# Turning x by DMA, starting the first expert units beside expert 0, pacing the weight loads, and loading expert 0's weights in fp32

## The chip, the core and the metric

The kernel runs on one NeuronCore of a Trainium2 chip. The metric is the device time of one execution in microseconds; the time of a version is the median of several runs. The engines named here are TensorE (PE in the profile, with PEld for its weight loads), VectorE (DVE), ScalarE (ACT), GpSimd (POOL) and SyncE (SP), which issues DMAs. POOL and ACT issue DMAs too, and a DMA that converts fp32 to fp16 on its way is issued by POOL in this kernel.

## The reference

Attention with a window of 32 and 32 global tokens, over 8 batches of 8 heads with 512 local tokens; its output, 4352 tokens of 512 numbers, goes through a mixture of eight experts with Sinkhorn routing.

```python
x = attention(q_l, k_l, v_l, q_g, k_g, v_g)      # [4352, 512], tokens b*544 + (32 global, 512 local)
P = np.exp(x @ w_gate)                           # [4352, 8]
for _ in range(8):
    P /= P.sum(1, keepdims=True); P /= P.sum(0, keepdims=True); P *= N / E
for e in range(8):
    out += P[:, e:e+1] * (np.maximum(x @ w1[e], 0) @ w2[e])   # w1: 512x1024, w2: 1024x512
```

Since P is positive, a token's row of x may be scaled by P before expert e's first product.

## The kernel before, in words

**The order of the work** is written by a small planner, not by hand. `op(...)` records an operation with its engine, an assumed duration, what it depends on and a key. `run_schedule` simulates the engines and emits the operation that can start first, the smaller key first among equals. Each engine then runs its instructions in that fixed order, and so does each queue of DMA issues; a late operand holds up everything behind it on the same engine.

**Front: attention.** 32 pairs of heads, four in a batch. For a pair: loads on SP's queue (`load`), casts to fp16 on DVE, eight PE transposes of q and k, evacuations, scores, exponentials on ACT, masks on DVE, `attend` on PE, and `normalise` on DVE (L297), which leaves the pair's output `xn` with tokens on partitions. The later products need x with its 512 features on partitions. So `back` (L329) turns the pair with four PE transposes into PSUM (`gbank`), a copy (L200) brings it to `xT`, one tile that holds x of all tokens, and `flip` (L335) with a copy at L527 does the same for the global tokens. `gate` (L339) multiplies x by w_gate, `exp_gate` writes K_nat.

**Expert 0** is computed densely and unscaled with fp16 weights in `w1_0` and `w2_0`, which two converting DMAs on POOL's queue load (`load_w0`, L540, behind a small POOL copy `tick` that waits for a q load of batch 1). Its units are the filler: `h_unit` (L388) makes one 128-feature slice of h for a group of 512 tokens, `y_unit` (L407) one 128-token slice of y, with keys from 1000, so that PE takes them wherever attention leaves it free. There are 560 such matmuls. y goes to DRAM (`y0d`, L422, on POOL's queue).

**Routing** is a chain of DVE steps with one small PE matmul in each of the eight rounds (L643 to L659, `colsum` L656). It starts when all gates are done and ends in P_nat. P is then turned on PE (L672) and stored to DRAM (`ptd`, L677), and x is stored from `xT` to `xTd` (L610).

**Back: experts 1 to 7.** The tokens are 17 groups of 256. Pass 0 runs experts 1, 2, 3 over all groups, pass 1 experts 4 to 7: 119 units (`work`). A unit is one expert on one group, by a scheme that needs seven block products in place of eight, for each of the two layers: `product1` (P1 to P7 of layer 1, eight matmuls of 128 columns each, L726) and `product2` (L764, four matmuls of 256 columns each). For a unit, `prep` on DVE scales x by P (two operations at L708, from `xg` and `pb`, which `load_group` L690 brings on SP's queue: x of the group, and the P of each expert broadcast to all partitions) and makes the sums `tt` (L97, L100). ACT copies partial sums out of PSUM (`snap`, L737) and does the relus (L740); DVE combines them. In layer 2 the accumulators in PSUM start from the output so far (`load_o` L771, `seed`), and `fin_...` and `store_o` (L936, SP's queue) end a group. `xp`, the scaled x of a unit, has three buffers; P3 is the last product that reads it, in the order written 6.2 + 3.53 us after its unit's P1.

**Weights of experts 1 to 7** come by converting DMAs on POOL's queue, four of 512 KB (written) for an expert: `load_w1` and `load_w2` (L85, L93). Experts 1 and 2 load during attention, 3 when attention's buffers are released, 4 and 5 early in pass 0. Experts 6 and 7 take the buffers of 1 and 2, so their loads wait for the last units of pass 0. `combine_w1` and `combine_w2` make sums of weight blocks on DVE.

The back is scheduled in a second call of `run_schedule`: its first unit is emitted after the last operation of expert 0, and only the `prep` of units 0 and 1 belongs to the first call.

Of the kernel before, what the change touches and what calls it, by code (L numbers as in the profile page):

```python
# [17 lines left out]
def kernel(  # L18
# [51 lines left out]
    identity32 = persist.tile([P, P], FP32)  # L70
    xT = fill.tile([P, DP, NTOK], FP16, bufs=1)
# [6 lines left out]
    xTd = dram.tile([GN, P, DP, 256], FP16)  # L78
    ws = {}

    def load_w1(e, pool, tag=""):
        w1r = pool.tile([P, 4, DK, F // 2], FP16, tag="w1r" + tag, bufs=1, name="w1r")
        src = moe_w1[e].rearrange("(dko dki) f -> dki dko f", dki=P)
        for f in (0, 1):
            nc.gpsimd.dma_start(out=w1r[:, 2 * f : 2 * f + 2].rearrange("p a k x -> p (a k) x"),  # L85
                                in_=src[:, :, F // 2 * f : F // 2 * (f + 1)])
        ws[e] = [w1r, None, None]

    def load_w2(e, pool, tag=""):
        wb = ws[e][1] = pool.tile([P, 7, FK, Dhalf], FP16, tag="wb" + tag, bufs=1, name="wb")  # L90
        src = moe_w2[e].rearrange("(fko fki) d -> fki fko d", fki=P)
        for c in (0, 1):
            nc.gpsimd.dma_start(out=wb[:, 2 * c : 2 * c + 2].rearrange("p a k x -> p (a k) x"),  # L93
                                in_=src[:, :, Dhalf * c : Dhalf * (c + 1)])
# [101 lines left out]
    qkT, ugk, u_, xns, ogs, pts, pss, pgs, pos_, pqs, hTs, phs, pys = ({} for _ in range(13))  # L196
# [100 lines left out]
    def normalise(p):  # L297
# [3 lines left out]
        t = xns[p] = wk.tile([P, NM, 2, Dh], FP16, tag="xn", bufs=3, name="xn")  # L301
# [4 lines left out]
    xo = gbank[:, 0:256].bitcast(FP16)  # L306
    ptg = gbank[:, 384 : 384 + 2 * Sg].rearrange("p (a s) -> p a s", s=Sg)
# [15 lines left out]
    def normalise_g(b, hh):  # L323
        rg = wk.tile([P, 1], FP32, tag="rg", name="rg")
        nc.vector.reciprocal(out=rg, in_=pog[:, Dh:VC])
        t = ogs[b, hh] = wk.tile([P, Dh], FP16, tag="og", name="og")
        nc.vector.tensor_scalar(out=t, in0=pog[:, 0:Dh], scalar1=rg[:, 0:1], scalar2=None, op0=ALU.mult)

    def back(p):  # L329
        for m in range(NM):  # L330
            nc.tensor.transpose(xo[:, P * m : P * (m + 1)], xns[p][:, m, :, :], identity)
# [7 lines left out]
    def gate(t0, t1):  # L339
        for to in range(t0, t1):  # L340
# [610 lines left out]
    for u in range(NW + 2):  # L951
# [10 lines left out]
        if 2 <= u < NW:  # L962
            add_prep(u)
# [31 lines left out]
```

## Time and profile before

| | |
|---|---|
| median of 3 runs | 1023.87 us (1021.98 to 1028.93) |
| the profiled execution: own time, span | 1021.38 us, 1019.7 us |
| mean granted TensorE clock | 0.990 |
| PE busy, PEld busy | 980.2 us (96%), 829.9 us (81%) |
| DVE, ACT, POOL busy | 884.6 us (87%), 671.7 us (66%), 51.8 us (5%) |
| moved by DMA | 119.18 MB, mean 117 GB/s |

The span runs from the first to the last instruction; the 1.7 us between it and the execution's own time lie around it. PE's busy time is modelled, since matmuls overlap in the array: an engine that is busy all the time may still start fewer matmuls than it could. The number of matmuls in a stretch says more.

### The profile page before, as it was taken

The page shows a single profiled execution, that of the slowest core. Times are in us where ns is not written, and L with a number is a line of the kernel's source. Part 1 is how long each engine was busy: PE and PEld are TensorE (multiplying, and loading weights), DVE is VectorE, ACT ScalarE, POOL GpSimd, SP SyncE. Part 2 cuts the span into 40 slices and gives each one's busy share as a digit, 9 for nine tenths or more (in the row PEclk, how much of TensorE's full clock was granted, in tenths as well). Part 3 has the DMA queues.
Part 4 walks back from the last instruction along what each step waited for, and adds up shares of the span by engine and source line. Part 5 has one row for each costly group of instructions (what it writes and reads, how often), then busy time and mean ns, then how long its engine had stood idle before and what let it go on. Part 6 is the DMA issues. An engine that isn't in the chain of part 4 may idle for free. (4 is left out here: it accounts for less than half of the span.)

```text
span 1019.7 us, 30644 instructions
## 1 busy us (share of the span) xinstructions
PE 980.2 (96%) x12921; PEld 829.9 (81%) x12921; DVE 884.6 (87%) x2058; ACT 671.7 (66%) x1306; POOL 51.8 (5%) x89
## 2 busy tenths in 40 slices
PE   5999999889999999999999889999999999999997
PEld 3556555434799999999999878999999999999997
DVE  5577776581599999999999899999999999999996
ACT  4678877434677766676776656666666666666664
POOL 2000130211300000000000100000000000000000
PEclk9799999989999999999999999999999999999999
DMA  9979696732962232232322891222222222222211
GB/s 272 256 219 307 193 215 126 144 103 100 229 140 85 94 94 89 90 94 93 108 73 79 153 195 60 88 73 74 74 74 73 75 74 74 74 75 73 75 43 43
DMA packets 127530, 119.18 MB, mean 117 GB/s; under 512 B 17424, under 2 KB 102944, under 8 KB 127392
## 3 DMA queue, kind: packets, MB, share of 16 engines
q1 hardware_dynamic: 99040, 91.13, 29.3%
q0 software_dynamic: 26768, 25.70, 13.4%
q8 instruction: 101, 1.65, 0.7%
q10 hardware_dynamic: 1584, 0.39, 0.2%
q14 instruction: 37, 0.30, 0.1%
HBM read 102.65 MB, written 31.33 MB: 131 GB/s over the span
## 5 line engine op out<-in xcount | busy, mean ns | idle before, releaser
L740 ACT ACTIVATE h<-h 128x512 f16<-128x512 f16 x357 | 224.2, 630 | 72.0 <-DVE h L100 70.1
L726 PEld LDWEIGHTS <-w1r 128*128 128x128 f16 x3808 | 244.9, 98 | 22.6 <-issue 13.7
L726 PEld LDWEIGHTS <-w1x 128*128 128x128 f16 x2856 | 182.3, 98 | 5.3
L764 PEld LDWEIGHTS <-s 128*128 128x128 f16 x1904 | 172.4, 98 | 15.9 <-DVE s L100 0.6
L708 DVE TENSOR_TENSOR xp<-xg,pb 128x512 f16<-128x512 f16 x238 | 163.0, 686 | 15.2 <-PE Y L726 15.0
L726 PE MATMUL X<-tt,w1r 128*128 128x128 f16 x1904 | 145.1, 219 | 7.4 <-ACT u3s L737 5.8
L764 PE MATMUL acc_4639<-wb,s 128*128 128x256 f16 x952 | 142.5, 273 | 0.3 <-DVE s L100 0.3
L764 PEld LDWEIGHTS <-h 128*128 128x128 f16 x1428 | 130.0, 98 | 12.6 <-issue 1.0
L737 ACT COPY u3s<-X 128x512 f32<-128x512 f32 x119 | 69.4, 583 | 73.7 <-PE X L726 73.4
L100 DVE TENSOR_TENSOR h<-p1s,Z 128x512 f16<-128x512 f32 x119 | 81.0, 681 | 29.5 <-ACT p1s L737 27.9
L737 ACT COPY p1s<-X 128x512 f32<-128x512 f32 x119 | 69.1, 580 | 29.1 <-PE X L726 29.1
L100 DVE TENSOR_TENSOR h<-u3s,Y 128x512 f16<-128x512 f32 x119 | 81.1, 681 | 2.1 <-ACT u3s L737 2.1
L737 ACT COPY u2s<-X 128x512 f32<-128x512 f32 x119 | 68.5, 576 | 21.5 <-PE X L726 21.4
L100 DVE TENSOR_TENSOR h<-u2s,Y 128x512 f16<-128x512 f32 x119 | 81.0, 680 | 1.6 <-PE Y L726 1.6
L740 ACT ACTIVATE h<-X 128x512 f16<-128x512 f32 x119 | 70.1, 589 | 17.0 <-PE X L726 14.0
L396 PE MATMUL ph<-xT,w_0_77 128*128 128x512 f16 (+1 forms) x288 | 74.0, 374 | 1.8 <-ACT ys L200 1.1
L726 PE MATMUL X<-xp,w1r 128*128 128x128 f16 x952 | 72.6, 219 | 1.9 <-DVE xp L708 1.7
L726 PE MATMUL Z<-xp,w1r 128*128 128x128 f16 x952 | 72.6, 219 | 1.1 <-DVE h L100 1.0
L726 PE MATMUL X<-tt,w1x 128*128 128x128 f16 x952 | 72.6, 219 | 0.0
L726 PE MATMUL Y<-tt,w1x 128*128 128x128 f16 x952 | 72.6, 219 | 0.0
L726 PE MATMUL Y<-xp,w1x 128*128 128x128 f16 x952 | 72.6, 219 | 0.0
L764 PE MATMUL acc_4636<-wb,s 128*128 128x256 f16 x476 | 71.4, 273 | 0.1
(985 smaller groups left out, 1651.1 us busy)
## 6 DMA issues: line engine op xcount, KB each, us to landing
pb<-ptd SPq DMA_DIRECT2D x119, 128.0 KB, 4.1
y0d<-ys POOLq DMA_DIRECT2D x34, 256.0 KB, 3.5
xg<-xTd SPq DMA_DIRECT2D x34, 256.0 KB, 3.7
o<-y0d SPq DMA_DIRECT2D x34, 256.0 KB, 2.8
ya<-o SPq DMA_DIRECT2D x34, 256.0 KB, 2.1
o<-ya SPq DMA_DIRECT2D x34, 256.0 KB, 3.0
out_dram<-o SPq DMA_DIRECT2D x34, 256.0 KB, 2.0
qs<-in_q_l_dram SPq DMA_DIRECT2D x7, 1024.0 KB, 6.9
```

Source lines behind the costliest of these rows:

```text
L100: nc.vector.tensor_tensor(out=o, in0=a, in1=b_, op=ALU.add)
L396: nc.tensor.matmul(phs[g, fm][:, 0:TG], w1_0[:, dk, P * fm : P * (fm + 1)], xT[:, dk, P * g0 : P * g0 + TG], start=(dk == 0), stop=(dk == ...
L708: nc.vector.tensor_tensor(out=x[:, ks], in0=xgs[n, g][:, ks], in1=pb.unsqueeze(1).broadcast_to([P, DK, 256]), op=ALU.mult)
L726: nc.tensor.matmul(dst[:, j, :], l[:, d, P * j : P * (j + 1)], r[:, d, :], start=(first and j == 0 and d == 0), stop=(j == FK - 1 and d == ...
L737: nc.scalar.copy(out=d[k], in_=X[k])
L740: nc.scalar.activation(out=hq(k, f, t), in_=hq(k, f, t) if src is None else src, func=AF.Relu)
L764: nc.tensor.matmul(acc(i), l[:, j, :], wb[:, r, j, :], start=(e == es[0] and j == 0 and i in (1, 5)), stop=(e == es[-1] and j == FK - 1), ...
```

## The change

It is made of five parts.

1. x is stored to DRAM with tokens on partitions (`xd`; `store_x` on POOL's queue, `store_xg` on SP's) and read back turned by a transposing DMA on SP's queue, 512 tokens at a time (`turn_group`), into `xTs`, three buffers of one group each. `back`, `flip` of the outputs, their copies, `xT` and `xTd` go.
2. For the units, x is scaled with tokens on partitions, where P is one number for each partition (`scale_x`, two operations on ACT or DVE), stored to one of four DRAM buffers (`put_x`) and read back turned (`turn_x`), both on SP's queue. The broadcast loads of P, its turn on PE and `ptd` go, and so do the two `prep` operations at L708.
3. Layer 1 of units 0 and 1, the preparation of units 0 to 3 and the first `load_o` are planned in the first call of `run_schedule`, beside expert 0.
4. Weights of experts 1 to 5 come in 16 pieces of 128 KB (written), still converting DMAs on POOL's queue; each piece first waits, with a small POOL copy, for the piece two before it, and in the back for a unit's x as well. Experts 6 and 7 are converted during pass 0 from DRAM to DRAM (`cast_piece`) and fetched at the end of the pass by four plain DMAs each on SP's queue (`load_half`). `load_o` and `store_o` move from SP's queue to POOL's.
5. Expert 0's weights are loaded in fp32 by SP's queue, eight pieces of 512 KB through three buffers, and converted by POOL (`cast_w0`).

Assumed durations in the planner's calls are part of the code and not measurements.

```diff
-    def load_w1(e, pool, tag=""):
-        w1r = pool.tile([P, 4, DK, F // 2], FP16, tag="w1r" + tag, bufs=1, name="w1r")
-        src = moe_w1[e].rearrange("(dko dki) f -> dki dko f", dki=P)
-        for f in (0, 1):
-            nc.gpsimd.dma_start(out=w1r[:, 2 * f : 2 * f + 2].rearrange("p a k x -> p (a k) x"),
...
+    def wait_for(v):
+        nc.gpsimd.tensor_copy(out=tick, in_=v)
+    def load_piece(e, i):
+
+        if len(landed) > 1:
+            wait_for(landed[-2])
+        if i < 8:
+            k, f = divmod(i, 2)
+            o = ws[e][0][:, 2 * f + k // DK, k % DK, :]
+            nc.gpsimd.dma_start(out=o, in_=moe_w1[e][P * k : P * (k + 1), F // 2 * f : F // 2 * (f + 1)])
+            landed.append(o[:, 0:1])
+        else:
+            k, c = divmod(i - 8, 2)
+            o = ws[e][1][:, 2 * c + k // 2, 2 * (k % 2) : 2 * (k % 2) + 2, :]
+            nc.gpsimd.dma_start(out=o, in_=moe_w2[e][2 * P * k : 2 * P * (k + 1), Dhalf * c : Dhalf * (c + 1)].rearrange(
+                "(k p) d -> p k d", p=P))
+            landed.append(o[:, 0, 0:1])
+
+    def cast_piece(e, i):
+        d, src, n = (wd1, moe_w1, D // 8) if i < 8 else (wd2, moe_w2, F // 8)
+        r = slice(n * (i % 8), n * (i % 8 + 1))
+        nc.gpsimd.dma_start(out=d[e][r], in_=src[e][r])
+
+    def load_half(e, i):
+        if i < 2:
+            nc.sync.dma_start(out=ws[e][0][:, 2 * i : 2 * i + 2].rearrange("p a k x -> p (a k) x"),
+                              in_=wd1[e].rearrange("(k p) f -> p k f", p=P)[:, :, F // 2 * i : F // 2 * (i + 1)])
+        else:
+            c = i - 2
+            nc.sync.dma_start(out=ws[e][1][:, 2 * c : 2 * c + 2].rearrange("p a k x -> p (a k) x"),
+                              in_=wd2[e].rearrange("(k p) d -> p k d", p=P)[:, :, Dhalf * c : Dhalf * (c + 1)])
...
-    def back(p):
-        for m in range(NM):
-            nc.tensor.transpose(xo[:, P * m : P * (m + 1)], xns[p][:, m, :, :], identity)
+    def store_x(b, hh):
+        r0 = S_tok * b + Sg
+        nc.gpsimd.dma_start(out=xd[r0 : r0 + Sl, 4 * Dh * hh : 4 * Dh * (hh + 1)].rearrange("(m p) d -> p m d", p=P),
+                            in_=xns[2 * b + hh].rearrange("p m i d -> p m (i d)"))
+
+    def store_xg(b):
+        for hq in range(4):
+            nc.sync.dma_start(out=xd[S_tok * b : S_tok * b + Sg].rearrange("s (h c) -> s h c", h=2)[:, :, Dh * hq : Dh * (hq + 1)],
+                              in_=ogs[b][Sg * hq : Sg * (hq + 1)])
...
+    def turn_group(g):
+        t0, n = groups[g]
+        xTs[g] = fill.tile([P, DP, n * P], FP16, tag="xT", bufs=3, name="xT")
+        nc.sync.dma_start_transpose(out=xTs[g], in_=xd[P * t0 : P * (t0 + n)])
...
-        BK[p] = op("PE", 0.24, lambda: back(p), k + 0.3, uses=[N[p]], alloc=("xo", 1), lat=PEL)
-        EB[p] = op(either(0.49, 0.61), 0, lambda eng: copy_on(eng, xT[:, hp, S_tok * b + Sg : S_tok * (b + 1)], xo), k + 0.3,
-                   uses=[BK[p]])
...
+            stored[b].append(op("DMA3", 0.7, lambda: store_x(b, hh), k + 0.5, uses=[N[p], N[p - 1]], lat=DMAL))
+            if hh:
+                stored[b].append(op("DMA", 0.3, lambda: store_xg(b), k + 0.5, [NG[b, 1]], uses=[NG[b, 0]], lat=DMAL))
...
-    def load_w0():
-        nc.gpsimd.tensor_copy(out=tick, in_=stage[1, "q"][:, 0, 0:1])
-        nc.gpsimd.dma_start(out=w1_0, in_=moe_w1[0].rearrange("(dko dki) f -> dki dko f", dki=P))
-        nc.gpsimd.dma_start(out=w2_0, in_=moe_w2[0].rearrange("(fko fki) d -> fki fko d", fki=P))
-
-    w0 = op("DMA", 12.0, load_w0, 3.6, [ops_load[1, "q", 0], ops_load[1, "k", 0]], lat=DMAL)
+    w0s = {}
+
+    def load_w0(i):
+        t = w0s[i] = ld.tile([P, F], FP32, tag="w0s", bufs=3, name="w0s")
+        if i < DP:
+            nc.sync.dma_start(out=t, in_=moe_w1[0, P * i : P * (i + 1)])
+        else:
+            nc.sync.dma_start(out=t.rearrange("p (a d) -> p a d", a=2),
+                              in_=moe_w2[0, 2 * P * (i - DP) : 2 * P * (i - DP + 1)].rearrange("(a p) d -> p a d", p=P))
+
+    def cast_w0(i):
+        o = w1_0[:, i] if i < DP else w2_0[:, 2 * (i - DP) : 2 * (i - DP + 1)].rearrange("p a d -> p (a d)")
+        nc.gpsimd.tensor_copy(out=o, in_=w0s[i])
+
+    w0 = []
+    for i in range(8):
+        l = op("DMA", 1.7, lambda i=i: load_w0(i), (3.4 if i < 4 else 3.8) + 0.01 * i, alloc=("w0s", 3), lat=DMAL)
+        w0.append(op("POOL", 0.95, lambda i=i: cast_w0(i), 3.4 + 0.01 * i, uses=[l]))
...
+                TG[g] = op("DMA", 2.0, lambda g=g: turn_group(g), k, [x for x in stored[b] + (stored[b - 1] if b else [])],
+                           alloc=("xT", 3), lat=5.5)
+                GA[g] = op("PE", 0.55, lambda g=g: gate(g), k + 0.1, alloc=("pl", 1), uses=[TG[g]], lat=PEL)
+                GE[g] = op("ACT", 0.2, lambda g=g: exp_gate(g), k + 0.1, uses=[GA[g]])
...
+            u0 = op("PE", us, lambda g=g, i=i: h_unit(g, i, 0), key, [*w0[:4], before],
+                    alloc=("mm", 2), uses=[htag, TG[g]])
...
     def load_group(n, g):
-        es = PASSES[n]
-        x = xgs[n, g] = late["cp"].tile([P, DP, 256], FP16, tag="xg", name="xg")
-        nc.sync.dma_start(out=x, in_=xTd[g])
-        t = pbs[n, g] = late["cp"].tile([P, 4, 2, P], FP32, tag="pb", name="pb")
-        for i, e in enumerate(es):
-            nc.sync.dma_start(out=t[:, i], in_=ptd[2 * g : 2 * g + 2, e, :].unsqueeze(0).broadcast_to([P, 2, P]))
+        x = xgs[n, g] = late["cp"].tile([P, 2, D], FP16, tag="xg", name="xg")
+        nc.sync.dma_start(out=x, in_=xd[256 * g : 256 * (g + 1)].rearrange("(a p) d -> p a d", p=P))
+    def scale_x(eng, k, a):
+        n, g, e = work[k]
+        if a == 0:
+            xss[k] = late["cp"].tile([P, 2, D], FP16, tag="xs", bufs=2, name="xs")
+        o, i, w = xss[k][:, a], xgs[n, g][:, a], P_nat[:, 2 * g + a, e : e + 1]
+        if eng == "ACT":
+            nc.scalar.activation(out=o, in_=i, func=AF.Copy, scale=w)
+        else:
+            nc.vector.tensor_scalar(out=o, in0=i, scalar1=w, scalar2=None, op0=ALU.mult)
+
+    def put_x(k):
+        nc.sync.dma_start(out=xsd[k % NX].rearrange("(a p) d -> p a d", p=P), in_=xss[k])
+
+    def turn_x(k):
+        xps[k] = late["cp"].tile([P, DP, 256], FP16, tag="xp", bufs=3, name="xp")
+        nc.sync.dma_start_transpose(out=xps[k], in_=xsd[k % NX])
...
-            nc.sync.dma_start(out=t[:, a, :], in_=src[2 * g + a])
+            nc.gpsimd.dma_start(out=t[:, a, :], in_=src[2 * g + a])
...
+    def piece(e, i, u):
+        if e < 6:
+            new_w(e, i, eC, str(e))
+        wait_for(xps[u][:, 0, 0:1])
+        (load_piece if e < 6 else cast_piece)(e, i)
+
+    def add_piece(n, u):
+        e, i = 4 + n // 16, n % 16
+        mk(("W", i), e, "DMA2", 1.4, lambda: piece(e, i, u), TU * (u - 0.5), [], [("TX", u)], lat=DMAL)
+        if e < 6 and i == 15:
+            add_combos(e, u + 8, lambda: eC, str(e), [(("W", j), e) for j in range(8)], [(("W", j), e) for j in range(8, 16)])
+
+    def add_switch(e, pool, xtag, u0, u1):
...
+            mk(("H", i), e, "DMA", 1.7, half, TU * (u0 - 3 + i // 2),
+               [(("W", j), e) for j in range(16)] + [(("H", i - 1), e)] * (i > 0) + ([("P3", u1), ("P4", u1)] if i < 2 else [(("A", j), u1) for j in range(1, 8)]), lat=2.5)
...
+        for a in (0, 1):
+            mk(("SC", a), k, {"ACT": 0.58, "DVE": 0.26}, 0, lambda eng, a=a: scale_x(eng, k, a), at, [("routed", 0)],
+               [("LG", k - PASSES[n].index(e))] + [(("SC", 0), k)] * a, alloc=("xs", 2) if a == 0 else None)
+        mk("PX", k, "DMA", 0.1, lambda: put_x(k), at + 1.0, [(("SC", 1), k)], [(("SC", 0), k)], ("xsd", NX), lat=2.3)
+        mk("TX", k, "DMA", 1.2, lambda: turn_x(k), at + TU, [], [("PX", k)], ("xp", 3), lat=2.3)
...
-        nc.sync.dma_start(out=(ya, outr)[c[0]][2 * c[1] + a], in_=obs[c][:, a, :])
-
+        nc.gpsimd.dma_start(out=(ya, outr)[c[0]][2 * c[1] + a], in_=obs[c][:, a, :])
...
+    def load_w(e, deps, pool):
+        for i in range(16):
+            mk(("W", i), e, "DMA", 1.3, lambda i=i: (new_w(e, i, pool()), load_piece(e, i)), 900.0 + e + 0.01 * i,
+               deps if i == 0 else [(("W", i - 1), e)], lat=DMAL)
...
+    for k in range(4):
+        add_prep(k)
+    add_o(c0, 0.0)
+    for k in (0, 1):
+        add_layer1(k)
+    run_schedule()
```

## The prediction

> **What bounds the kernel now.** First I read the busy time of each engine by stretches, then the chain of work that ended last, then the waits in the stretches that fall short, then groups and DMA issues.
>
> ```profile
> 900.00:910.00 10.00, 10.00 (x134) 9.44 (x133) 9.89 (x24) 7.27 (x13) 0.00 (x0) 1.00 0.56 186
> 200.00:210.00 10.00, 5.30 (x17) 2.15 (x17) 7.01 (x17) 1.67 (x3) 0.54 (x1) 0.70 0.70 147
> 230.00:240.00 10.00, 10.00 (x47) 4.47 (x46) 3.88 (x8) 5.34 (x9) 1.62 (x3) 1.00 0.39 141
> 262.00:540.00 278.00, 275.34 (x3712) 257.83 (x3709) 271.87 (x641) 195.80 (x372) 6.80 (x9) 1.00 0.39 104
> 540.00:640.00 100.00, 91.71 (x1211) 84.18 (x1209) 94.78 (x221) 60.98 (x116) 6.50 (x8) 1.00 0.56 122
> 700.00:1000.00 300.00, 300.00 (x4078) 284.62 (x4076) 285.78 (x670) 201.97 (x376) 0.00 (x0) 1.00 0.23 74
> ```
>
> Columns: stretch, length, busy time and number for PE, PEld, DVE, ACT and POOL, granted clock, DMA share, GB/s. From 700 to 1000 us PE starts 4078 matmuls; a unit has 84, so it takes 300/(4078/84) = 6.18 us. The chain there is PE alone:
>
> ```profile
> 959.93 0.44 PE acc_4639 L764 x4
> 960.37 0.45 PE X L726 x8
> ```
>
> Seven products of 0.44 and seven of 0.45 make 6.2 us again: pass 1 is at PE's own pace, and faster DVE work gains nothing there. 119 units at 6.18 us are 735.4 us; the back runs from 260.6 to 1014.2 us, so 18 us of it are holes. At 13.6 matmuls per us, pass 0 (3712 in 278 us) is short of 5 us and the change of passes (1211 in 100 us) of 11 us. In expert 0's tail a full stretch has 47 matmuls and the one at 200 us has 17: 6.4 us. Its cause is in the timeline:
>
> ```profile
> 204.90 0.69 DVE L97 TENSOR_TENSOR wb<-wb 128x1024 f16<-128x1024 f16 x1 [2.19 <-DMA wb<-in_moe_w_dram]
> 206.19 0.59 PE L656 MATMUL pcs<-cp,ones_sc 128*128 128x8 f32 x2 [3.83 <-DVE cp L651]
> 568.40 1.50 POOL L85 DMA_DIRECT2D w1r<-in_moe_w_dram  x2 [299.27 <-PE X L726]
> ```
>
> DVE waited for a weight load with the routing step behind it, PE for the routing, and the clock fell to 0.70. At the change of passes the loads of experts 6 and 7 cannot be issued before the buffers are free (568 us) and come late.
>
> **The change, part by part,** against the profiled execution's 1021.4 us.
>
> (a) Turns removed. In the front PE is dense too: 127.5 of 130 us busy from 60 to 190 us. Removed are 128 transposes and 32 flips.
>
> ```profile
> L331 PE MATMUL gbank<-identity,xn 128*128 128x128 f16 x128 | 13.3, 230 | 3.6 <-DVE og L327 1.7 <-DVE xn L302 1.7
> L200 ACT COPY xT<-gbank 128x512 f16<-128x512 f16 x30 | 17.7, 590 | 10.0 <-PE gbank L337 6.0 <-PE gbank L331 3.8
> ```
>
> A 128-column matmul costs 0.45/8 = 0.056 us of PE, so 7.1 us, and 32 short ones at half of it 0.9: -8. Ends: 0, if ACT and DVE set the front's pace, and -13 by busy time. I take -8, since expert 0 fills what attention leaves. The 17.7 us of copies are ACT's, which is not full; I count none.
>
> (b) Routing hole. The C2 sums of experts 1 and 2 still go to DVE inside the chain, but the loads are smaller and earlier. Take -6.4; ends 0 and -7.
>
> (c) Hand-off. `xTs` has three buffers, so group 8 is turned only when h of group 5 is done, the 344th of 560 filler matmuls. Before, 273 were issued by 187 us, so routing starts 71 x 0.213 = 15 us of filler later. That costs PE nothing, but leaves 216 (some at half width), or 43 us, as cover. Behind it lie routing, 188.2 to 220.0 us (32; 27 without the hole), scaling (two ACT operations like L740, 0.63 each, 1.3), put and turn. Put: 2.0 to 5.4 us (stores `out_dram`, `xTd`). Turn: no row shows a transposing DMA; the nearest, the 256 KB load `xg`, lands in 3.7 us, one under load took 7.6. Sum 34 to 46 us against 43. The middle of the sum is covered, its upper quarter not: take +1.5; ends 0 and +8, where the waiting PE drops its clock as at 200 us. With the routing hole closed, this is the wait that is late next.
>
> (d) Pass 0. DVE is 98% busy there. It loses 2 x 0.69 us a unit; if scaling goes to ACT, ACT rises from 202/300 x 6.18 = 4.2 to 5.4 us of 6.18. Take -4.5 of 5; ends 0 and -5.
>
> (e) Change of passes. Experts 6 and 7 come as 512 KB plain loads; 4 MB at the 306 GB/s of the front (8 to 14 us) are 13 us for both; before, they took from 568 us to some 600 (last issue 586.5, landing 13.3). Take -10; ends 0 and -11.
>
> (f) Start. DMA is full to 44 us, and what comes first matters.
>
> ```profile
> 14.99 8.99 SPq L208 DMA_DIRECT2D qs<-in_q_l_dram  x1
> 25.36 1.42 DVE L200 CAST kn<-ks 128x512 f16<-128x512 f32 x4
> 26.44 0.61 PE L227 MATMUL pt<-identity,qn 128*128 128x128 f16 x4
> ```
>
> SP's queue holds a later load for 9 us already. Three of the eight new pieces, 1.5 MB, go ahead of batch 1's q and k by their keys (3.4 against 3.5): 4.9 us at 306 GB/s. Batch 1's first pair starts on PE 1 us after its casts, and no filler runs before 43 us, so PE would idle; the fourth piece waits on SP for a buffer, with loads behind it. Against that, the converting loads of the same 4 MB go (landing 13.9 and 21.3 us). POOL's eight conversions cost at most four times the 0.40 us of L359, 12.8 us on an engine idle from 20 to 48 us. Take +2; ends -3 and +6.
>
> (g) End. The last store leaves from POOL: `y0d` from there lands in 2.9 us, `out_dram` from SP in 2.0, and issuing costs 0.54 against 0.4. Take +1.5; ends +1 and +2.
>
> (h) Queues in the back. SP loses 119 `pb` issues and gains a put and a turn per unit, each holding what stands behind it: a late put holds the next turns, a late turn the next puts and group loads. POOL gets 1.5 pieces a unit in pass 0 (0.71 for the copy `tick`, 0.78 to 0.91 for the DMA) and four `o` transfers a group at 0.54: 3.1 of 6.18 us. The piece's copy reads `xp`, so a late POOL holds the turn three units on. 0 as long as a turn lands in time; otherwise the first rival.
>
> Sum: 1021.4 - 8 - 6.4 + 1.5 - 4.5 - 10 + 2 + 1.5 = 997.5. The median before lies 2.5 us above the profiled execution, the lowest run 0.6; I add 1.5: **999 us**.
>
> The Trainium skill has a price for the turn. "DMA: Bandwidth & Descriptors", section "Latency and other measured facts", gives a transposing DMA 261 GB/s; with the 2 us fixed cost of "Anatomy of one DMA" that is an estimate of 3.0 us for 256 KB, by which (c) would be 0 and the sum 996. No row here shows it.
>
> A rule speaks against the change. POOL's issues at 568.40 us took 0.75 us each with DVE busy for 10.00 of the 10 us after 570; `y0d` took 0.54. The Trainium skill, "SBUF — State Buffer", section "SBUF: two separate sides", says that a DVE operation that holds the port shared with GpSimd keeps GpSimd from writing descriptors, some 3.1 us in place of 0.62 in its example. By that, 2.8 POOL transfers a unit would be 8.7 us, 2.5 over a unit, or some 105 us over the 42 units that carry pieces. The row shows nothing of the kind, so I go by the row.
>
> **The rivals.** *Turns come late* (slower). With three buffers, unit u+3 is turned after P3 of unit u, and P3 ends 6.2 + 3.5 + 0.45 = 10.2 us after its unit's P1. If a turn takes L us from then to landing, three units last 10.2 + L: up to L = 8.3 it is free, above that each us costs 119/3 = 39.7 us, and the gain of 24 is gone at 8.9. At L = 10 it is 999 + 67 = 1066. For it: no row has a transposing DMA, `pb` once took 10.7 us and `xg` 7.6, and in pass 0 pieces share the DMA engines. Against: medians of 3.7 and 4.1 us, and a DMA share of 0.23 that the new traffic raises by about 0.75 MB a unit, 2.5 us at 306 GB/s.
>
> *The front gives back what the back gains.* Batch 1 late by its full 4.9 us plus a blocked queue (+6), hand-off +8, routing hole half closed: 999 + 4 + 6.5 + 3.2 = 1013. For it: PE falls below 9 of 10 us busy in most stretches to 40 us, and the 43 us of cover meet a sum of 34 to 46. Against: from 60 us on filler absorbs delays.
>
> *The change of passes stays open.* The eight plain loads are on the same queue as puts and turns, and 13 us of DMA hold them: (e) is 0, 1009. Against: they are asked for two to three units, 12 to 18 us, before use.
>
> **How the numbers follow.** Forecast 0.66, front 0.16, passes 0.05, late turns 0.13. A measurement of this kernel tells about 1%, 10 us, from no change. Faster by more (under 1013.6): the forecast, under half of the front's case, most of the third: 0.77. Within: 0.08. Slower: late turns and the front's bad end, 0.15. The forecast's own range is 986 (better ends of a, c, d, e and f) to 1014 (two or three terms at their worse ends). The range 983 to 1024 leaves out 0.06 below and most of the late turns and the front's bad end, some 0.14, above; 983 lets several better ends fall together with a median as near the profiled execution as the lowest run is.
>
> **What would show it.** Right: units of 6.18 us with matmul counts near 136 per 10 us through pass 0 and the change of passes; no stretch in expert 0's tail under 40 matmuls; first P1 within 2 us of the last filler matmul; DVE under 85% in the back; no PE wait on a DMA into `xp`. (a) is right if attention's stretches hold more filler. Wrong: waits of PE or DVE on `xp`, SP's queue waiting on P3 or POOL for several us a unit, batch 1's first pair after 31 us, a clock under 1.00 near the hand-off.

## The result, and the profile after

The changed kernel takes **1107.91 us** (median of 4 runs, 1104.59 to 1111.54), the kernel before 1025.13 us beside it (4 runs). The ratio is 1.081, with a 95% interval of 1.075 to 1.086. I had forecast 999 us, and 983 to 1024 as the range: the kernel is not faster but slower by 83 us. The profiled execution took 1111.54 us (span 1109.8, mean granted clock 0.976). Of the versions below, `e2_true_latency` and `e1c_latency_and_buffers` each had one execution far out of line (1965.83 and 1081.03 us), which their ratios leave out.

First the same stretches as before, from the view of busy time by stretches, in the same columns; pass 0 is cut at 280 us, since layer 1 now starts at 271.2 us.

```profile
900.00:910.00 10.00, 10.00 (x138) 9.43 (x136) 8.25 (x22) 7.67 (x15) 2.17 (x4) 1.00 0.64 189
200.00:210.00 10.00, 10.00 (x48) 4.50 (x47) 0.00 (x0) 5.34 (x9) 6.31 (x13) 1.00 0.73 117
210.00:220.00 10.00, 5.54 (x32) 2.16 (x30) 0.00 (x0) 1.98 (x4) 2.56 (x5) 0.67 0.82 186
280.00:540.00 260.00, 231.15 (x2930) 210.17 (x2928) 189.34 (x468) 182.42 (x342) 82.78 (x181) 0.97 0.79 158
540.00:640.00 100.00, 89.40 (x1181) 82.28 (x1179) 73.74 (x188) 68.99 (x130) 21.59 (x48) 1.00 0.71 152
700.00:1000.00 300.00, 288.91 (x3879) 270.73 (x3877) 240.06 (x610) 206.14 (x380) 24.34 (x45) 1.00 0.55 133
```

The kernel before, in the same stretch of pass 0:

```profile
280.00:540.00 260.00, 258.95 (x3467) 242.46 (x3465) 257.44 (x611) 181.83 (x345) 0.00 (x0) 1.00 0.33 97
```

DVE is relieved as forecast (189 of 260 us in pass 0; before, it was 98% busy). The hole at 200 us is closed (48 matmuls for 17), but a new one follows it: from 210 to 220 us 32 matmuls start, at a granted clock of 0.67. PE stands there 4.5 us at a gate until a group's turned x (`xT`) lands, and 8.2 us at two gates in all:

```profile
PE gbank L386 <- DMA xT<-xd: 8.2, 2, 4.5
```

In the back PE isn't fuller. From 280 to 540 us it starts 2930 matmuls, where the kernel before starts 3467 in the same stretch. From 280 to 700 us, in three stretches, 4798 stand against 5500, and at 13.6 per us that is 52 us lost; from 700 to 1000 us 3879 against 4078, 15 us. Pass 1, which was at PE's own pace, is now below it.

So the back has a new wait, and the groups of instructions name it (busy time and mean ns | idle time ahead of the group, and what ended it):

```profile
L796 PE MATMUL acc_4712<-wb,s 128*128 128x256 f16 x952 | 144.8, 275 | 35.6 <-DVE s L126 25.9 <-DVE o L129 5.7 <-DVE s L129 3.8
L126 DVE TENSOR_TENSOR tt<-xp 128x512 f16<-128x512 f16 x119 | 50.3, 423 | 96.4 <-DMA xp<-xsd_82 38.0 <-DMA xp<-xsd_80 23.8 <-DMA xp<-xsd_81 19.9
```

DVE stands for 96 us in all ahead of the first sum `tt` of a unit, until the turned x (`xp`) lands. PE waits little for `xp` (2.5 us); it waits for `s`, DVE's sums for layer 2. The timeline of pass 0 shows how the one makes the other (start, duration, what ended the idle time):

```profile
399.98 2.20 SPq L735 DMA_TRANSPOSE xp<-xsd_82  x1
...
402.63 0.42 DVE L126 TENSOR_TENSOR s<-s,h 128x512 f16<-128x512 f16 x1
...
408.48 0.43 DVE L126 TENSOR_TENSOR tt<-xp 128x512 f16<-128x512 f16 x1 [5.43 <-DMA xp<-xsd_82]
...
408.82 0.42 DVE L126 TENSOR_TENSOR s<-h 128x512 f16<-128x512 f16 x1
...
409.30 1.03 PE L796 MATMUL acc_4712<-wb,s 128*128 128x256 f16 x4 [4.01 <-DVE s L126]
...
410.13 1.06 PE L758 MATMUL X<-tt,w1r 128*128 128x128 f16 x8
```

The turn is issued at 399.98 and lands 8.5 us later. The `tt` that it feeds belongs to a unit whose first product starts only at 413.5 us; but DVE's order is fixed, and the sum `s`, which an earlier unit does need, stands behind it. PE idles 4.0 us. Then it is slow besides: four matmuls take 1.03 us for 0.60, while the granted clock is 0.50 (from 408 to 414 us; 0.90 from 414 to 418).

### The profile page after: what moved, and what is told of

It is laid out like the page before. It is cut to its first block, busy times and chain, and to the rows that moved or that the text cites. A ratio compares the mean times of both kernels' runs of the same rounds, so it can differ in the third digit from the quotient of the medians.

```text
span 1109.8 us, 31187 instructions
## 1 busy us (share of the span) xinstructions
PE 1000.1 (90%) x12758; PEld 834.2 (75%) x12758; DVE 798.0 (72%) x1954; ACT 716.7 (65%) x1360; POOL 226.3 (20%) x470
## 4 chain that ended last, share of the span: by engine, by line
PE 30%; DMA 17%; DVE 6%; issue 5%; SPq 1%; ACT 1%; POOL 1%; POOLq 0%; DVEq 0%; ACTq 0%
PE X L758 8%; PE Y L758 5%; DMA xp<-xsd_82 5%; PE acc_4711 L796 4%; PE acc_4712 L796 4%; DMA xp<-xsd_80 4%; PE acc_4709 L796 3%; DVE h L129 3%; DMA xg<-xd 2%; DMA xp<-xsd_79 2%; DMA xp<-xsd_81 2%; PE Z L758 2%; PE acc_4710 L796 2%; DVE tt L126 1%; SPq L735 1%
## 5 line engine op out<-in xcount | busy, mean ns | idle before, releaser
L758 PEld LDWEIGHTS <-w1r 128*128 128x128 f16 x3808 | 252.3, 99 | 22.4 <-issue 10.9
L758 PEld LDWEIGHTS <-w1x 128*128 128x128 f16 x2856 | 189.1, 99 | 29.7 <-issue 22.7
L796 PEld LDWEIGHTS <-s 128*128 128x128 f16 x1904 | 168.8, 99 | 55.8 <-DVE s L126 30.2
L796 PE MATMUL acc_4712<-wb,s 128*128 128x256 f16 x952 | 144.8, 275 | 35.6 <-DVE s L126 25.9
L796 PEld LDWEIGHTS <-h 128*128 128x128 f16 x1428 | 128.7, 99 | 11.8 <-issue 1.6
L126 DVE TENSOR_TENSOR tt<-xp 128x512 f16<-128x512 f16 x119 | 50.3, 423 | 96.4 <-DMA xp<-xsd_82 38.0
L958 POOL DMA_DIRECT2D out_dram<-o x34 | 18.7, 551 | 333.6 <-DVE tt L129 286.1
L726 ACT ACTIVATE xs<-xg,P_nat 128x512 f16<-128x512 f16 x100 | 71.4, 721 | 13.2 <-DMA xg<-xd 11.7
L796 PE MATMUL acc_4709<-wb,h 128*128 128x256 f16 x476 | 72.8, 276 | 0.8 <-ACT acc_4709 L811 0.2
```

What stands on the lines that cost most here:

```text
L126: nc.vector.tensor_tensor(out=o, in0=a, in1=b_, op=ALU.subtract)
L726: nc.scalar.activation(out=o, in_=i, func=AF.Copy, scale=w)
L758: nc.tensor.matmul(dst[:, j, :], l[:, d, P * j : P * (j + 1)], r[:, d, :], start=(first and j == 0 and d == 0), stop=(j == FK - 1 and d == ...
L796: nc.tensor.matmul(acc(i), l[:, j, :], wb[:, r, j, :], start=(e == es[0] and j == 0 and i in (1, 5)), stop=(e == es[-1] and j == FK - 1), ...
L958: nc.gpsimd.dma_start(out=(ya, outr)[c[0]][2 * c[1] + a], in_=obs[c][:, a, :])
```

## The experiments

Times are medians; a ratio is to the kernel before, run beside it on the same chip, with a 95% interval. A run without a ratio is a single execution.

### Ring or order

Two theories: the turn can't start earlier, because `xp` has three buffers (my rival); or the order was written for a turn that lands sooner than it does. The planner reckoned 1.2 + 2.3 = 3.5 us from issue to landing.

```diff
-        xps[k] = late["cp"].tile([P, DP, 256], FP16, tag="xp", bufs=3, name="xp")
+        xps[k] = late["cp"].tile([P, DP, 256], FP16, tag="xp", bufs=4, name="xp")
... and bufs=4 for tt, ("xp", 4) for the planner
```

> The changed kernel with four buffers instead of three for xp, the turned scaled x of a unit, and four for tt, the sums made from it; the planner knows of both. A turn may then start a unit earlier, 6.2 us, than right after P3 of the unit whose buffer it takes. Theory 'ring': the turns start at P3, land in 4.3 us (median) to 9.9, and DVE, whose order is fixed, waits 96 us for them with the sums that PE needs behind it; a unit more of lead removes most of that, so DVE's waits on xp fall from 96 us to under 30, pass 0 and pass 1 lose 40 to 60 of their 67 us, and the time is 1050 to 1070. Theory 'contention' (the weight pieces fill the DMA engines in pass 0 and would make any turn late): only pass 1 gains, time 1085 to 1100, waits on xp above 60 us. Theory 'queue' (a turn waits on SP's queue behind puts and loads that wait themselves): the turn's own wait moves to the put, time above 1090.

Measured: **1109.6 us** (1.083, 1.078 to 1.088). The waits:

```profile
DVE tt L126 <- DMA xp<-xsd: 71.3, 43, 5.9
```

No gain, and DVE still waits 71 us. The ring is not what binds, and the 1050 to 1070 of theory 'ring' fell. The time is one that 'queue' allows, but the wait didn't move as it says: from 280 to 1000 us SP stood 256 us at the turns and 283 us at the puts, against 217 and 331 in the changed kernel.

```diff
-        mk("TX", k, "DMA", 1.2, lambda: turn_x(k), at + TU, [], [("PX", k)], ("xp", 3), lat=2.3)
+        mk("TX", k, "DMA", 1.2, lambda: turn_x(k), at + TU, [], [("PX", k)], ("xp", 3), lat=6.0)
```

> Only the planner's assumed latency of a unit's turn is changed, from 2.3 to 6.0 us beyond its 1.2 us of issue; the buffers and all instructions stay, so only the order written differs: DVE's sums from xp are put later among its other work. Theory 'order' (DVE stands at the sums of a unit that is not needed yet, while sums for earlier units stand behind them): DVE's waits on xp fall from 96 to under 50 us and the time to 1070 to 1090. Theory 'ring' (with three buffers the turn can't start earlier and the unit is late whatever the order): within 10 us of the changed kernel, 1098 to 1118, with the waits moved from DVE to PE.

Measured: **1066.8 us** (1.041, 1.039 to 1.044), 41 us less. The instructions are the same; only their order differs, on every engine and queue, since the planner writes all of them. DVE's wait for `xp` falls from 96 to 22 us, and pass 1 is back at 4055 matmuls in its 300 us.

```profile
L126 DVE TENSOR_TENSOR tt<-xp 128x512 f16<-128x512 f16 x119 | 49.9, 419 | 22.3 <-DMA xp<-xsd 22.2
```

With both edits:

> Both edits so far: the planner's latency of a turn at 6.0 us, and four buffers for xp and for tt. With the true latency alone the kernel took 1066.8 us, with four buffers alone 1109.6. Theory 'order only': buffers add nothing, 1060 to 1072. Theory 'ring behind order' (the waits that are left in pass 0, PE and DVE on xp, come from turns that can't start before P3 frees a buffer): the fourth buffer now takes another 10 to 20 us, 1045 to 1057.

Measured: **1066.2 us** (1.041, 1.038 to 1.044): buffers add nothing, 'order only'.

### Traffic, or the order again

With the true latency of the turn, 280 to 700 us still lacked 360 matmuls, 26 us. Is it the DMA engines, 0.8 busy, or the order?

```diff
-                add_piece(npc, u)
+                pass
... add_switch(6, ...) and add_switch(7, ...) go; ws[4..7] = ws[1], ws[2], ws[3], ws[1]
```

> The changed kernel without any load of the weights of experts 4 to 7 in the back: the 64 pieces and eight half loads are left out with the small POOL copies ahead of them, and experts 4 to 7 use the weights of 1, 2, 3 and 1, so the output is another. The sums of weight blocks for them go as well (DVE has less to do). Theory 'contention': pass 0 and the change of passes recover 40 us or more, the median landing of a turn there falls from above 4 to near 3 us, time 1055 to 1068. Theory 'ring': the turn lands some 1 us earlier at most and pass 0 keeps more than half of its 47 us, time 1080 to 1100. Pass 1 keeps its 20 us under both.

Measured: **1071.5 us**: 36 us less, between the two expectations, so it decided nothing alone. On top of the true latency:

> The kernel with the planner's latency of a turn at 6.0 us, and without the loads of the weights of experts 4 to 7 in the back and their sums (they use the weights of 1, 2, 3 and 1, so the output is another). With the latency alone it took 1066.8 us, without the loads alone 1071.5. Pass 0 and the change of passes then still miss some 26 us against the kernel before. Theory 'contention is what is left': 1040 to 1050, all but 5 us of the 26 gone. Theory 'same loss, taken away twice' (the loads only made the turns late, and the order now allows for that): 1058 to 1068.

Measured: **1036.5 us**. All of the 26 us goes. And the transposing itself:

```diff
-        nc.sync.dma_start_transpose(out=xps[k], in_=xsd[k % NX])
+        nc.sync.dma_start(out=xps[k].rearrange("p (a b) t -> p a (b t)", a=2), in_=xsd[k % NX].rearrange("(a p) d -> p a d", p=P))
```

> The changed kernel with the unit's transposing DMA replaced by a plain load of the same 256 KB, so x is not turned for the units and the output is another; all buffers, waits and the order stay. It gives the price of the transposing itself. Theory 'transposing': a plain load is issued by SP in 0.1 us or less instead of 1.23 and lands 1 us or more earlier, and the time falls by 40 us or more, to 1050 to 1068. Theory 'ring and order': a load that starts at P3 is nearly as late as a turn that does, DVE still waits 60 us or more, time 1080 to 1105.

Measured: **1065.7 us**, as much as the true latency brings. SP's issue falls from 1.23 to 0.36 us, the landing in pass 0 from 4.8 us (in the kernel with the true latency) to 4.1. That removes little of the latency, and yet 42 us of time, which fits the order: a landing nearer to the assumed 3.5 us helps. So I gave the planner the other two latencies that it had too short, and had the group's x asked for a unit earlier:

```diff
-    mk("LG", k, "DMA", 0.1, lambda: load_group(n, g), at - TU, [("open", 0)], alloc=("xg", 2), lat=2.5)
+    mk("LG", k, "DMA", 0.1, lambda: load_group(n, g), at - 2 * TU, [("open", 0)], alloc=("xg", 2), lat=6.0)
-    mk("PX", k, "DMA", 0.1, lambda: put_x(k), at + 1.0, ..., ("xsd", NX), lat=2.3)
+    mk("PX", k, "DMA", 0.1, lambda: put_x(k), at + 1.0, ..., ("xsd", NX), lat=4.5)
```

> On the kernel with the planner's latency of a turn at 6.0 us (1066.8 us): the planner also assumes 6.0 instead of 2.5 us for the load of a group's x and asks for it a unit earlier, and 4.5 instead of 2.3 us for the store of the scaled x (under load they took 4.1 and 3.8 in the median). What is left in pass 0 begins, in that kernel's trace, with ACT or DVE standing at the scaling until a group's x lands (2.24 us at 428 us), after which PE runs at 0.73 of its clock. Theory 'order, again': pass 0 gains another 10 to 20 us, 1045 to 1057. Theory 'contention alone': the order can't help while the DMA engines are 0.83 to 0.86 busy, 1062 to 1070.

Measured: **1036.8 us** (1.015, 1.010 to 1.019): the same as with no weight traffic at all, and below what either theory said. This kernel moves every byte of the changed one. Its stretches, DVE's wait, and its landings from 280 to 540 us:

```profile
280.00:540.00 260.00, 257.21 (x3470) 241.49 (x3468) 227.89 (x582) 199.69 (x377) 89.45 (x207) 1.00 0.90 185
540.00:640.00 100.00, 97.62 (x1295) 91.48 (x1293) 88.83 (x221) 73.97 (x139) 15.07 (x32) 0.98 0.79 191
700.00:1000.00 300.00, 300.00 (x4079) 284.60 (x4078) 241.64 (x618) 226.74 (x425) 25.96 (x48) 1.00 0.55 138
```

```profile
L126 DVE TENSOR_TENSOR tt<-xp 128x512 f16<-128x512 f16 x119 | 49.6, 417 | 4.2 <-DMA xp<-xsd 4.2
```

```profile
xsd<-xs SPq DMA_DIRECT2D x43, 256.0 KB, 4.0
xg<-xd SPq DMA_DIRECT2D x14, 256.0 KB, 3.8
xp<-xsd SPq DMA_TRANSPOSE x41, 4.9
```

The DMA engines are busier than in the changed kernel (0.90 for 0.79) and a turn lands no sooner (4.9 us in the median; in the changed kernel 4.5 to 5.7, by DRAM buffer), but little waits: DVE's 96 us are 4, and PE starts 3470 matmuls for 2930. 71 of the 83 us were the order. Two more runs look at the traffic, on the kernel with the true latency of the unit's turn. With the pieces, but without the sums and the half loads:

> On the kernel with the planner's latency of a turn at 6.0 us: the 64 pieces of experts 4 to 7 are loaded or converted as before, with their waits on GpSimd, but the sums of weight blocks on DVE and the eight half loads at the change of passes are left out, and experts 4 to 7 use the weights of 1, 2, 3 and 1 (another output). With the latency alone it took 1066.8 us, without the pieces as well 1036.5. Theory 'DMA traffic': the pieces cost the 30 us by what they do to the DMA engines, 1055 to 1066. Theory 'the sums': 32 sums of 0.6 to 0.7 us on DVE, and their place in its order, cost most of it, 1036 to 1046.

Measured: **1070.7 us**: what the pieces cost in that order they don't cost by DVE's sums. Whether by the DMA engines or by the waits that they put on GpSimd's queue, this run doesn't separate. With the weights of 4 to 7 loaded as before, in 512 KB bursts:

> On the kernel with the planner's latency of a turn at 6.0 us (1066.8 us): the weights of experts 4 to 7 come as in the kernel before, by converting DMAs of 512 KB (written) without GpSimd's waits, 4 and 5 in two short bursts in pass 0, and 6 and 7 at the change of passes when the buffers are free. Theory 'contention of the pieces': pass 0 loses little outside the bursts and gets some 25 us back, the change of passes loses its 11 us again, time 1048 to 1058. Theory 'it is the same bytes': the bursts stop the turns for 10 us or more each, 1066 to 1085.

Measured: **1071.1 us** (1.048, 1.044 to 1.052). The pieces are no worse than the bursts, against the first theory: the bursts cost pass 0 its stretches around 300 and 400 us (387 matmuls from 380 to 420 us, for 544 at 13.6 per us), and the change of passes has a hole again, of 15 us (339 matmuls from 620 to 660 us, for 546 in the kernel with all latencies true).

### The front

What is left, some 15 us, is lost ahead of 280 us, and 2.4 us after the last matmul: from 280 to 1000 us the kernel with all latencies true starts 9656 matmuls, the kernel before 9571. Seven runs look at it, the first three on the kernel with the true latency of the unit's turn alone. The first matmuls of expert 0, from the view of one tile (`ph`, up to 190 us), before and after:

```profile
L396 PE MATMUL ph<-xT,w_0_77 x160: 376/379/631, 43.2 to 188.8; 128*128 128x512 f16 x160
```

```profile
L438 PE MATMUL ph<-xT,w_0_75 x136: 376/379/634, 63.8 to 185.3; 128*128 128x512 f16 x136
```

The filler starts 21 us later, and with `py` 234 of its matmuls have run by 190 us, for 285: 51 x 0.217 = 11 us. SP's queue in the changed kernel (timeline):

```profile
9.61 8.63 SPq L583 DMA_DIRECT2D w0s<-in_moe_w_dram  x4
18.28 0.43 SPq L237 DMA_DIRECT2D qs<-in_q_l_dram  x1
...
32.65 2.62 SPq L366 DMA_DIRECT2D xd<-og  x4
35.37 5.38 SPq L585 DMA_DIRECT2D w0s<-in_moe_w_dram  x4
40.81 0.46 SPq L237 DMA_DIRECT2D qs<-in_q_l_dram  x1
...
44.88 10.20 SPq L381 DMA_TRANSPOSE xT<-xd  x1
```

Batch 1's q goes out at 18.28 us (before, 9.49), batch 2's at 40.81 (before, 14.99), behind a store that waits for DVE and the second half of `w0`; a group turn then holds the queue for 10.2 us. The first edit undoes part 5, the second takes the store off SP's queue as well:

```diff
-    w0 = eight loads by nc.sync.dma_start in fp32, eight casts by nc.gpsimd.tensor_copy
+    w0 = [op("DMA", 12.0, load_w0, 3.6, [ops_load[1, "q", 0], ops_load[1, "k", 0]], lat=DMAL)]   # as in the kernel before
```

> The kernel with the planner's latency of a turn at 6.0 us (1066.8 us), with part 5 undone: expert 0's weights come again by two converting DMAs on GpSimd's queue behind its small copy, as in the kernel before. Theory 'SP's queue in the front' (four 512 KB pieces stand ahead of batch 1's q and k, and four more hold the queue until a buffer is free): batch 1's first pair starts on PE near 26 to 28 us instead of 31.7, the first filler runs before 50 us instead of 64, time 1050 to 1060. Theory 'other causes' (stores of x's global tokens and turns of groups hold the queue): less than 4 us, 1063 to 1069.

Measured: **1078.5 us** (1.053, 1.046 to 1.059), 12 us worse. The filler starts at 59.9 us, hardly earlier: it is not the fp32 weights that delay it. Layer 1 starts at 280.8 us for 271.6, so 9 of the 12 us are lost ahead of it. Part 5 is the better way in this front.

```diff
-            nc.sync.dma_start(out=xd[S_tok * b : S_tok * b + Sg].rearrange("s (h c) -> s h c", h=2)[...], in_=ogs[b][...])
+            nc.gpsimd.dma_start(...)
```

> As the run before it (planner's latency 6.0 us, expert 0's weights as before), and besides, the stores of the global tokens' x (four small DMAs a batch) move from SP's queue to GpSimd's. In the changed kernel SP stands at such a store from 23.1 to 32.6 us, waiting for DVE, with loads behind it. Theory 'the store holds the loads': a further 5 to 12 us beside the kernel without this edit, 1042 to 1055. Theory 'no': within 4 us of it.

Measured: **1071.9 us** (1.048, 1.044 to 1.053), 6.6 us less than without it, though the intervals overlap. The group turns as plain loads (other data, so expert 0 and the gates compute on x that isn't turned):

> On the kernel with the planner's latency of a turn at 6.0 us (1066.8 us): the nine transposing DMAs of 512 tokens that turn x for expert 0 become plain loads of the same bytes, so x isn't turned for expert 0 and the gates, and the output is another. Each held SP's queue 2 to 10 us, with the loads of the next batch behind it. Theory 'the turn itself': SP's issue falls below 1 us, first filler before 56 us instead of 64, the 20 us that the front lost are halved or better, time 1050 to 1058. Theory 'the way through DRAM' (store, then load, whatever its kind, is what makes the filler late): 1060 to 1069.

Measured: **1056.6 us** (1.033, 1.027 to 1.040), 10 us less than 1066.8, though the intervals just touch and the filler still starts at 64.1 us. In the profiled executions layer 1 starts at 266.9 us for 271.6. The rest shows in the back (5272 matmuls from 280 to 700 us for 5133), where the edit changes no instruction, so not all of it is the front's. The next run is on the kernel with all latencies true, with the store of the global tokens on GpSimd's queue:

> On the kernel with true latencies in the back (1036.8 us): the stores of the global tokens' x move from SP's queue to GpSimd's; expert 0's weights stay on SP's queue in fp32. Theory 'SP's queue': the second half of expert 0's weights and batch 2's q no longer wait until 33 to 41 us behind a store, the front gains 6 to 12 us, 1025 to 1031. Theory 'the way through DRAM': the first filler still comes at 58 us or later, within 4 us, 1033 to 1041.

Measured: **1031.1 us** (1.008, 1.007 to 1.010), the best version of the changed kernel that I ran; it doesn't beat the kernel before. The filler starts at 65.0 us there too. The first group by PE (`back`, `flip` and the copies of the kernel before, for tokens 0 to 511):

> On the kernel with true latencies in the back (1036.8 us): the first group of 512 tokens is turned on PE, as in the kernel before (16 transposes, 4 flips and their copies), and the other eight still by DMA. Theory 'the way through DRAM': expert 0's first filler starts near 45 us instead of 64 and fills some 9 us of the stretch from 40 to 60 us, 1025 to 1030. Theory 'SP's queue': the filler that starts early is missing later, because the turns that follow are as late as before, 1033 to 1038.

Measured: **1037.3 us** (1.013, 1.010 to 1.016): no gain. The filler starts at 36.1 us, but by 190 us 229 of its matmuls have run, no more than the 234 of the kernel with all latencies true. Both edits, and a fourth buffer for group turns on the best version:

> Both edits: the first group turned on PE, and the global tokens' stores on GpSimd's queue, with true latencies in the back (1036.8 us with neither). If the two losses are separate, the gains add: 1015 to 1024. If they are one loss seen twice: not under the better of the two by more than 3 us.

> On the best version of the changed kernel so far (true latencies in the back, the global tokens' stores on GpSimd's queue, 1031.1 us): four buffers instead of three for the turned groups. Theory '(c)': a group is turned up to 13 us of filler earlier, the last gates come before 225 us instead of 233, routing ends earlier, and the hand-off loses 3 to 8 us less, 1023 to 1028. Theory 'not the buffers' (SP's queue, or attention's end, sets when the last group is turned): 1029 to 1034.

Measured: **1048.5 us** (1.024, 1.022 to 1.027) and **1049.4 us** (1.026, 1.020 to 1.032), both far off. Their waits, `m5_both` and then `n2_four_group_buffers`:

```profile
PE gbank L396 <- DMA xT<-xd: 16.0, 4, 6.8
```

```profile
PE gbank L386 <- DMA xT<-xd: 21.6, 4, 11.8
```

PE stands up to 11.8 us at a gate until a group's turn lands, with the filler behind the gate; in the best version it was 6.8 us in all. The planner reckons 2.0 + 5.5 us for a group turn; in the changed kernel its issue alone took 1.7 to 10.2 us, and it landed in 7.2 us in the median. This could be the same fault as in the back, one stage earlier, but the traces support it only in part. In `n2_four_group_buffers` the two longest waits (11.8 and 7.0 us) are for turns that landed 13.1 and some 11.5 us after issue. In `m5_both` the longest (6.8 us) is for a turn that landed in 8.9 us, 1.4 past the 7.5 reckoned, and the medians (5.5 and 5.8 us) lie inside it. A run with that latency corrected was not made, so the cause of these two losses stays open.

### Two terms of the sum by themselves

On the kernel before: weights of experts 6 and 7 converted early and fetched by plain loads, and the C2 sums of experts 1 and 2 behind the routing chain.

```diff
+            op("DVE", 0.605, lambda n=n: combine_w2(e, n), key, [a, chain[-1]])
+        if 6 <= u < 38:
+            add_piece(u - 6, u)
... add_switch(6, ...) and add_switch(7, ...) for add_late_w(6, ...) and add_late_w(7, ...)
```

> The kernel before, with two terms of my sum alone and x turned on PE as it was: the weights of experts 6 and 7 are converted during pass 0 from DRAM to DRAM by GpSimd, one piece of 128 KB a unit from unit 6 on, and fetched at the change of passes by plain DMAs; and the C2 sums of experts 1 and 2 come after the routing chain. My terms (e) and (b) say -10 and -6.4: 1003 to 1010. If the change of passes is bound by the plain loads as well, (e) is under 4: 1012 to 1018. If the pieces disturb pass 0 as they did in the changed kernel (DMA share there is only 0.37, so I don't expect it): 1018 or more.

Measured: **1026.8 us** (1.003, 1.002 to 1.005). It is not faster. The change of passes:

```profile
540.00:640.00 100.00, 93.40 (x1215) 85.52 (x1214) 95.21 (x220) 61.36 (x118) 0.00 (x0) 0.98 0.37 115
```

1215 matmuls, for 1211 before, though DVE waits only 0.7 us for those weights. DVE is as busy as it was (95.2 for 94.8). The routing hole did shrink (146 matmuls from 190 to 220 us, for 105). Pass 0 lost what that gained (3352 matmuls from 280 to 540 us for 3467): at 373.9 us a load of the output so far is issued, soon after two 512 KB weight loads and a piece; ACT waits 6.7 us for it, and PE 5.0 us behind ACT. Then the sums of weight blocks of experts 6 and 7 by GpSimd:

```diff
-            mk(("C1", n), e, "DVE", 0.605, lambda n=n: combine_w1(...), ...)
+            mk(("C1", n), e, "POOL", 1.2, lambda n=n: on_pool(lambda: combine_w1(...)), ...)   # C2 too
```

> On the kernel before with early weights for experts 6 and 7 and late C2 sums (1026.8 us): the sixteen sums of weight blocks of experts 6 and 7 go from DVE to GpSimd. Theory 'DVE bounds the change of passes': 16 x 0.65 us leave DVE there, the 10 us that are short of full pace from 590 to 640 us fall under 4, time 1017 to 1022. Theory 'transfers bound it': within 3 us, 1024 to 1030. GpSimd may also be too slow for the sums to be in time (more than 2 us each): 1028 or more.

Measured: **1045.3 us** (1.022, 1.018 to 1.026), 18.5 us more than with early weights alone. The timeline from 600 us:

```profile
600.13 0.42 DVE L121 TENSOR_TENSOR s<-s,h 128x512 f16<-128x512 f16 x1
...
600.38 2.15 POOL L124 TENSOR_TENSOR w1x<-w1r 128x1024 f16<-128x1024 f16 x1 [10.97 <-PE Z L750]
...
601.07 1.75 DVE L121 TENSOR_TENSOR s<-h 128x512 f16<-128x512 f16 x1
...
605.00 2.60 DVE L732 TENSOR_TENSOR xp<-xg,pb 128x512 f16<-128x512 f16 x1
...
607.53 0.67 DVE L124 TENSOR_TENSOR h<-u2s,Y 128x512 f16<-128x512 f32 x1
```

A sum takes GpSimd 2.1 us or more, and while it runs DVE's own sums take 1.75 to 2.60 us for 0.42 to 0.69. So this run doesn't settle whether DVE bounds the change of passes; it replaced one load on DVE by another.

## Why the prediction was wrong, point by point

Against the profiled execution before (1021.4 us) the profiled one after is 90 us longer: about 16 us ahead of 280 us, 52 from 280 to 700, 20 in the rest of pass 1 (15 of it up to 1000 us), and 2.5 from the start of the last matmul on (8.3 us for 5.8).

**Term (h), queues in the back, is the step that failed.** It was 0 "as long as a turn lands in time", and I judged "in time" by the ring: free up to 8.3 us after P3. The turns keep to that in the median (4 to 5 us from issue), and the fourth buffer shows that the ring is idle slack. The deadline that counted stood in the diff, where I read past it: 1.2 us of issue and `lat=2.3`. A fixed order puts the users of a transfer at the assumed landing, and a later landing stalls whatever stands behind them on that engine. By that 3.5 us, a median of 4.9 in pass 0 is late in more than half of the units. Size: 41 us for the turn, 30 more for the group's x (asked for a unit earlier besides) and the put, 71 of the 83 us. The rival *Turns come late* had the right symptom (DVE and SP's queue waiting around `xp` and P3), but its mechanism and its 39.7 us for each us are wrong: 33% more buffers bought nothing.

The Trainium skill's figure that I had beside it ("DMA: Bandwidth & Descriptors", "Latency and other measured facts", 261 GB/s for a transposing DMA) gave an estimate of 3.0 us. It was stretched: the page has that figure from one kernel, for a non-contiguous middle dimension. The runs have 3.6 us in the median in pass 1 of the kernel with the true latency, where the DMA engines are 0.55 busy, and 4.8 to 4.9 in pass 0; a plain load of the same bytes takes 3.3 and 4.1. By that estimate 3.5 us would have been safe, and it was not.

**(a), (b), (c), (f), the front and the hand-off,** summed to -10.9 and measured about +16. (b) was right for the hole that it named: it closed, and 29.4 us of routing ran through (232.8 to 262.2 us). But a new one opened from 210 to 220 us, at a gate that waits for a turned group, and the 8.2 us of PE at such gates stand in no term. (a) counted eight us of transposes and no delay; but x by way of DRAM puts the filler from 43 to 64 us and turns that hold SP's queue into the front; plain loads in their place brought 10 us, of which 4.7 show in the start of layer 1. In (f) batch 1's first pair moved from 26.4 to 31.7 us, inside what I had listed as its worse end, but batch 2's loads moved by 26 us, and of those I had said only "loads behind it". That fp32 weights cost the front was wrong in sign: with them undone the kernel took 12 us more. (c): the last gate comes at 232.8 us for 187.9, 45 us later, where I had 15; attention itself ends 12 us later (last `attend` matmul at 196 us for 184), and 51 filler matmuls fewer are done. Layer 1 starts 10.6 us later, for which I had +1.5 and an end of +8. The rival *The front gives back* had the mechanism and half the size: +14 over my forecast, measured some 27.

**(d)** was right once the order was: pass 0 at 3470 matmuls in 260 us is full pace (before 3467), and DVE is busy there for 228 us, not 257. **(e)** had the wrong cause. The changed kernel with true latencies starts 1295 matmuls from 540 to 640 us for 1211, 6 us, not 10; but early weights alone bring none of it. DVE's 94.78 of 100 us stood in the row that I quoted, and I blamed the transfers. In the changed kernel DVE has less to do: 138 scalings of 0.35 us in all, where it had two operations of 0.69 us for each of 119 units. That this is what closes part of the hole is likely, but no run isolates it. The rival *The change of passes stays open* held in the changed kernel itself: 1181 matmuls start there, fewer than the 1211 before. **(g)** was +1.5 and is +2.5.

**The rule that spoke against the change** didn't bite, as the row had said: GpSimd's 40 issues at L107 took 698 to 723 ns each with DVE running.

## What to carry to other kernels

Where an order of instructions is fixed ahead of time, every assumed latency is a deadline. Before you cost a change that adds transfers, put each assumed latency beside the landing that the trace shows under load, and ask what stands behind the consumer on its engine; more buffers don't mend an order, and a number on the long side cost nothing that could be seen here (7.2 us reckoned for a median of 4.9, with pass 0 at full pace). And where an engine is 95% busy in a stretch, test that before you blame the transfer that lands there.

## What the runs showed of the hardware that I had not expected

- A transposing DMA of 512 tokens held SP's queue for 1.7 to 10.2 us at issue, 4.1 in the median; a plain load of the same bytes 0.37 us in the median, but up to 7.3. For 256 tokens the least is 1.23 us against 0.36.
- Two-input sums on GpSimd slow DVE down: 128x512 sums with both inputs in SBUF took 1.75 to 2.60 us for 0.42 to 0.69, while those with an input in PSUM kept their 0.41 to 0.68. "SBUF — State Buffer" of the Trainium skill, "Who interferes with whom" and "SBUF: two separate sides", says this: such an operation and one of GpSimd that reads SBUF exclude each other. I had quoted the second section for the descriptors, where the 40 issues above show nothing of it, and not for the sums, where the run agrees.
- A pause of PE costs twice: after 4.0 us without work, ahead of 409 us, eight matmuls took 1.06 us for 0.61, at a granted clock of 0.50.
